# Weight loads from the fourth pair on go to ScalarE's DMA queue, each behind the cast of another pair

## Chip, core and metric

The kernel runs on one core of a Trainium2 chip. The metric is the device time of one execution in microseconds, the median of three runs. All times below are microseconds unless marked otherwise. TensorE is PE in the rows, VectorE DVE, ScalarE ACT, GpSimd POOL and SyncE SP.

## What is computed

A windowed attention, a gated MLP behind an RMS norm, and a second MLP, on 2304 tokens of 512 features (the reference, cut):

```python
scores = (1 / sqrt(D)) * q @ k.T                    # 4 batches, 8 heads, 576 positions, D = 64
scores = where((rel >= 0) & (rel < 64), scores, -1e9)
attn = exp(scores - max); attn = attn / (sum(attn) + 1e-9)
x = (attn @ v) as [2304 tokens, 512]
xn = x / sqrt(mean(x * x) + 1e-6) * rms_g
g = xn @ w_gate; val = xn @ w_val                   # 512 x 1536
x = (g * sigmoid(g) * val) @ w_out                  # 1536 x 512
h = x @ w_in; out = (h * sigmoid(1.702 * h)) @ w_out2   # 512 x 2048, 2048 x 512
```

The weights lie in HBM in 64-bit floats; everything else is 32-bit.

## The kernel before

**Blocks and passes.** The tokens are cut into blocks of 384 columns (three tiles of 128). The first MLP is made in two passes over half of its 1536 hidden features each; a pass goes through the blocks j = 0 to 5. The first pass also makes the attention of block j+1 while TensorE multiplies for block j: scores (`ps_s`, L271), exps (L301), transposes (`ps_t`, L321) that ScalarE copies to `pt` (L233), the product with v (`ps_v`, L336), then the norm (`ps_r`, L367 to L377), and at the end of the block the split of x into a high part `xh` (L385, L387) and a low part `xl` (L389). Each product of the MLPs is made of three passes of high and low parts (L396 for gate `psg`, value `psv` and `psh`; L531 and L622 into `acc`).

**Weights.** A weight chunk of 128 columns is 512 KB in HBM. Two chunks make a pair, and 34 pairs are used in a fixed order (`w_order`): gate and value of one feature chunk, the same of the next, the output rows of both, and so on, then the second MLP. Pairs are numbered from 0 here, so the fourth pair is pair 3. A pair goes through these steps:

- `w_load`: two DMAs of 512 KB into a staging tile `st` (three buffers). L117.
- `w_step`: ScalarE scales the two halves of the words (L144, L145), VectorE joins them into `m` (L146, L147, L150). There is one `m`.
- `w_half`, called at the start of the next step: ScalarE casts `m` to the high part of `w` (L128), VectorE subtracts to get the low part (L129).

In block 0 of the first pass nine pairs are prepared, one behind the other, since every weight is needed for the first time; later blocks and passes prepare the rest beside TensorE's work.

**Who issues loads.** Every DMA of the kernel is issued by SyncE, in one order: loads of q, k and v (L206), weight loads (L117), the store of x (L424), and at the end of a block four stores `o` of the block's result (L607) from two staging tiles `x2s` (ScalarE L606 for columns 0 and 2, VectorE L604 for 1 and 3), so the third `x2s` waits until the first store has landed. The first three pairs are loaded early, from `load_some`. The load of pair i+3 is called in `w_step` behind the join of pair i, and its staging tile is the one that the join of pair i has just read: it waits for that L150. What stands behind it in SyncE's order waits too, and it waits for what stands ahead.

**Order of the work.** A scheduler that knows the tiles, their buffers and the calls of `issue_after` writes out each engine's order when the program is built. Each engine then runs its own order and waits on semaphores.

Of the kernel before, what the change touches and what calls it, by code (L numbers as in the profile page):

```python
# [8 lines left out]
F32 = mybir.dt.float32  # L9
# [13 lines left out]
def window_attention__gated_mlp__mlp_kernel(  # L23
# [13 lines left out]
    nc = tc.nc  # L37
# [61 lines left out]
    w_next = [0, 0]  # L99
# [3 lines left out]
    def w_src(kind, f):  # L103
        c = slice(f * 128, (f + 1) * 128)
        if kind in "gvh":
            w = {"g": w_gate, "v": w_val, "h": w_in2}[kind]
            return w[:, c].bitcast(I32).rearrange("(k p) f -> p k f", p=128)
        return {"o": w_out, "p": w_out2}[kind][c, :].bitcast(I32)

    def w_load(limit):  # L110
        while w_next[0] < min(limit, n_w):
            pair = w_order[w_next[0]]
            w_next[0] += 1
            st = stp.tile([128, 2, 1024], I32, tag="st", name="st")
            for e, (kind, f) in enumerate(pair):
                dst = st[:, e, :].rearrange("p (k f) -> p k f", k=KC) if kind in "gvh" else st[:, e, :]
                nc.sync.dma_start(out=dst, in_=w_src(kind, f))  # L117
            staged.append(st)

    def after(ins):  # L120
        return tc.issue_after(ins) if ins is not None else nullcontext()

    def w_half():
        if not half:
            return
        pair, w24 = half.pop()
        w = wp.tile([128, 2, 1024], F32R, tag="w", name="w")
        nc.scalar.copy(w[:, 0, :], w24.bitcast(F32))  # L128
        nc.vector.tensor_tensor(w[:, 1, :], w24.bitcast(F32), w[:, 0, :].bitcast(F32), ALU.subtract)  # L129
        for e, key in enumerate(pair):  # L130
            weights[key] = w[:, :, e * 512:(e + 1) * 512]

    def w_step(limit):
        w_half()
        if w_next[1] >= min(limit, n_w):
            return
        w_load(w_next[1] + 1)
        pair = w_order[w_next[1]]
        w_next[1] += 1
        st = staged.pop(0).rearrange("p e (f two) -> p (e f) two", two=2)  # L140
        lo, hi = st[:, :, 0], st[:, :, 1]
        m = tmp.tile([128, 1024], I32, tag="tmp", name="m")
        with after(hold[0]):
            nc.scalar.mul(hi.bitcast(F32), hi.bitcast(F32), 2.0 ** -112)  # L144
            nc.scalar.activation(lo, lo.bitcast(U32), AF.Copy, scale=2.0 ** -29)  # L145
        nc.vector.tensor_scalar(m.bitcast(U32), hi.bitcast(U32), 3, None, ALU.logical_shift_left)  # L146
        nc.vector.scalar_tensor_tensor(  # L147
            m.bitcast(U32), hi.bitcast(U32), 0x80000000, m.bitcast(U32), ALU.bitwise_and, ALU.bitwise_or
        )
        nc.vector.tensor_tensor(m, m, lo, ALU.add)  # L150
        half.append((pair, m))
        w_load(w_next[1] + 2)


    NLD = 4
# [24 lines left out]
    def load_some():  # L180
        while ld_next[0] < len(ld_order):
            i = ld_next[0]
            if i >= N_FIRST + NLD and ld_order[i - NLD] not in ld_done:
                return
            kind, m = ld_order[i]
            ld_next[0] += 1
            if N_FIRST <= i <= N_FIRST + 2:
                w_load(i - N_FIRST + 1)
            if i < N_FIRST:
                t = part_tile().rearrange("p (h d) -> p h d", h=H)  # L190
            else:
                t = at.tile([128, H, D], F32, tag="qkv", name="qkv", bufs=NLD)
            ld_tile[kind, m] = t
            if kind == "v":
                if m == 0:
                    nc.vector.memset(t[64:128], 0.0)
                    rr = [(0, 64, 0, 0)]
                elif m % 4 == 0:
                    rr = [(64 * e, 64) + divmod((m - e) * GB, S) for e in range(2)]
                else:  # L200
                    rr = list(runs((m - 1) * GB, 128))
            else:
                rr = list(runs(m * 128, 128))
            src = {"q": q, "k": k, "v": v}[kind]
            for off, n, b, s in rr:
                nc.sync.dma_start(out=t[off:off + n], in_=src[b, :, s:s + n, :].rearrange("h s d -> s h d"))  # L206
# [264 lines left out]
    if True:  # L471
# [30 lines left out]
        for m in range(T0 // 128):  # L502
            att_S(m)
            if m + 1 < T0 // 128:
                att_Tk(m + 1)
                att_Tq(m + 1)
        hold[0] = last_exp[0]
        w_step(1)
        for m in range(T0 // 128):
            att_PT(m)  # L510
# [10 lines left out]
        for ps_i in range(2):  # L521
            f_lo, f_hi = ps_i * FH, (ps_i + 1) * FH
            for j in range(NB):
# [15 lines left out]
                def extras(f, i):  # L539
                    s = 3 * (f - f_lo) + i  # L540
                    if ps_i == 0:
                        for fn in slots.pop(j * NS + s, ()):
                            fn()
                        if j == 0:
                            if s % 2 == 0:
                                w_step(n_wh)
                        elif s % 9 == 8:
                            w_step(n_w1)
                    elif not end:
                        if s % 9 == 2:  # L550
                            w_step(n_w)
                    else:
                        w_step(n_w)
# [141 lines left out]
```

## Time and profile before

| | |
|---|---|
| time, median of 3 runs | 1029.68 (1028.36 to 1031.18) |
| time of the profiled execution | 1027.21 |
| its span | 1025.4 |
| mean granted clock of TensorE | 0.979 |
| TensorE busy | 987.4 (96%) |
| VectorE busy | 517.4 (50%) |
| ScalarE busy | 408.7 (40%) |
| moved by the one DMA queue of the kernel | 87.44 MB |

The span is the time from the first to the last instruction of the profiled execution; its time is 1.8 longer for what lies around it. Busy shares are means over stages that differ: block 0 of the first pass ends at about 125, the first pass with attention runs to about 350, and the rest is matmuls with little beside them.

### The profile page before, as it was taken

To read this page: it belongs to the slowest core of one execution; us is meant where nothing else is said; L and a number is where in the kernel's file an instruction comes from. 1 tells how busy PE (TensorE), PEld (TensorE's weight loads), DVE (VectorE), ACT (ScalarE), POOL (GpSimd) and SP (SyncE) were. 2 spreads that over 40 slices of the span, in tenths; PEclk is the share of its full clock that TensorE was granted. 3 is DMA by queue.
4 is the path that set the end of the run, shared out by engine and by line. 5 is a ranking of instruction groups with operands and counts; after the bars stand their busy time and mean duration, and the time that the engine had idled before them with its cause. 6 is when DMAs were issued, how large, how long until landed. Compare 5 with 4: busy or idle time off the path is not lost.

```text
span 1025.4 us, 15454 instructions
## 1 busy us (share of the span) xinstructions
PE 987.4 (96%) x6158; PEld 917.1 (89%) x6158; DVE 517.4 (50%) x1132; ACT 408.7 (40%) x884; POOL 12.2 (1%) x39
## 2 busy tenths in 40 slices
PE   7888999999989999999999999999999999999997
PEld 5877798988989899999999998998989989999996
DVE  5597756655575655656543688332232322322222
ACT  7586654654554333333332365222222222322222
POOL 2000000000000000000000000000000000000000
PEclk9698999999999999999999999999999999999999
DMA  9648644444361512423411352010010000000000
GB/s 233 184 124 212 181 102 133 101 86 135 83 186 42 196 66 87 165 72 122 157 72 63 113 171 77 1 62 1 1 62 1 32 31 1 31 1 1 32 1 31
DMA packets 113320, 88.43 MB, mean 86 GB/s; under 512 B 77664, under 2 KB 104288, under 8 KB 113248
## 3 DMA queue, kind: packets, MB, share of 16 engines
q1 hardware_dynamic: 113248, 87.44, 29.4%
q8 instruction: 48, 0.79, 0.3%
q14 instruction: 24, 0.20, 0.1%
HBM read 68.55 MB, written 18.87 MB: 85 GB/s over the span
## 4 chain that ended last, share of the span: by engine, by line
PE 83%; DVE 6%; ACT 5%; DMA 4%; issue 1%; SPq 0%; POOL 0%; DVEq 0%; ACTq 0%
PE acc L622 20%; PE psh L396 19%; PE acc L531 13%; PE psg L396 12%; PE psv L396 12%; PE ps_s L271 2%; PE ps_v L336 2%; ACT p L301 1%; PE ps_t L321 1%; DMA st<-in_moe_w_in_dram 1%; DMA st<-in_moe_w_val_dram 1%; DVE xraw L377 1%; ACT st L145 1%; DMA o<-x2s 1%; PE ps_r L367 1%
## 5 line engine op out<-in xcount | busy, mean ns | idle before, releaser
L638 DVE TENSOR_TENSOR a<-a,psh 128x384 f32<-128x384 f32 x96 | 53.0, 553 | 201.9 <-ACT a L637 201.9
L396 PE MATMUL psh<-x2h,w 128*128 128x384 f32 x768 | 153.3, 339 | 0.9 <-DVE a L638 0.6
L622 PE MATMUL acc<-w,gh 128*128 128x512 f32 x576 | 152.9, 397 | 0.0
L396 PEld LDWEIGHTS psh<-x2h,w 128*128 128x128 f32 x768 | 137.2, 188 | 4.3 <-DVE a L638 0.9
L637 ACT ACTIVATE a<-psh 128x384 f32<-128x384 f32 x96 | 47.0, 491 | 220.4 <-PE psh L396 217.2
L622 PEld LDWEIGHTS acc<-w,gh 128*128 128x128 f32 x576 | 107.1, 188 | 18.5
L531 PE MATMUL acc<-ah,w 128*128 128x384 f32 x576 | 117.6, 344 | 3.6 <-ACT w L128 3.3
L531 PEld LDWEIGHTS acc<-ah,w 128*128 128x128 f32 x576 | 103.5, 190 | 4.9 <-ACT w L128 3.7
L565 DVE SCALAR_TENSOR_TENSOR a<-a,psg 128x384 f32<-128x384 f32 x72 | 39.7, 552 | 115.5 <-ACT a L562 115.3
L396 PE MATMUL psh<-x2l,w 128*128 128x384 f32 x384 | 86.2, 338 | 0.0
L622 PE MATMUL acc<-w,gl 128*128 128x512 f32 x288 | 85.1, 396 | 0.0
L642 DVE TENSOR_TENSOR gl<-a,gh 128x384 fp32r<-128x384 f32 x96 | 53.4, 557 | 50.5 <-ACT gh L641 42.7
L562 ACT ACTIVATE a<-psg 128x384 f32<-128x384 f32 x72 | 35.1, 487 | 107.7 <-PE psg L396 107.7
L396 PEld LDWEIGHTS psh<-x2l,w 128*128 128x128 f32 x384 | 69.9, 188 | 5.9
L641 ACT CAST gh<-a 128x384 fp32r<-128x384 f32 x96 | 49.3, 513 | 62.5 <-DVE a L638 49.7
L396 PE MATMUL psg<-xh,w 128*128 128x384 f32 x288 | 65.3, 357 | 6.4 <-DVE a L565 2.6
L622 PEld LDWEIGHTS acc<-w,gl 128*128 128x128 f32 x288 | 54.2, 189 | 12.5
L531 PE MATMUL acc<-al,w 128*128 128x384 f32 x288 | 64.8, 343 | 0.0
L572 ACT CAST ah<-a 128x384 fp32r<-128x384 f32 x72 | 36.8, 511 | 70.1 <-DVE a L569 69.9
L396 PE MATMUL psv<-xh,w 128*128 128x384 f32 x288 | 62.9, 346 | 0.0
L396 PEld LDWEIGHTS psg<-xh,w 128*128 128x128 f32 x288 | 51.3, 193 | 11.4 <-DVE a L565 3.6
L301 ACT ACTIVATE p<-p,sm 128x128 f32<-128x128 f32 x128 | 49.6, 391 | 23.6 <-DVE sm L289 23.6
(104 smaller groups left out, 1433.6 us busy)
## 6 DMA issues: line engine op xcount, KB each, us to landing
st<-in_moe_w_out_dram SPq DMA_DIRECT2D x28, 512.0 KB, 4.3
o<-x2s SPq DMA_DIRECT2D x48, 192.0 KB, 3.4
st<-in_moe_w_in_dram SPq DMA_DIRECT2D x16, 512.0 KB, 5.0
st<-in_moe_w_gate_dram SPq DMA_DIRECT2D x12, 512.0 KB, 4.9
st<-in_moe_w_val_dram SPq DMA_DIRECT2D x12, 512.0 KB, 5.6
qkv<-in_v_dram SPq DMA_DIRECT2D x20, 256.0 KB, 4.2
x<-xraw SPq DMA_DIRECT2D x6, 768.0 KB, 4.7
xr<-x SPq DMA_DIRECT2D x6, 768.0 KB, 4.4
```

Source lines behind the costliest of these rows:

```text
L271: prev = nc.tensor.matmul(banks[e][64 * g:64 * g + 64, hp * 128:(hp + 1) * 128], QT[64 * e:64 * e + 64, hp, 64 * g:64 * g + 64], KT[64 * e ...
L301: last_exp[0] = nc.scalar.activation(p[e][:, hp, :], p[e][:, hp, :], AF.Exp, bias=sm[:, 0, i:i + 1], scale=-1.0, accum_out=sm[:, 1, i:i + ...
L396: nc.tensor.matmul(ps[:, :T], w[:, wi, c * 128:(c + 1) * 128], xx[:, c, :T], start=(i == 0), stop=(i == 3 * KC - 1),)
L531: nc.tensor.matmul(acc[c][:, :T], w[:, wi, c * 128:(c + 1) * 128], aa, start=(f == f_lo and pi == 0), stop=(f == f_hi - 1 and pi == 2),)
L562: tanh = nc.scalar.activation(a, psg[:, :T], AF.Tanh, scale=0.5).ins
L565: nc.vector.scalar_tensor_tensor(a, a, 1.0, psg[:, :T], ALU.add, ALU.mult)
L572: nc.scalar.copy(ah, a)
L622: nc.tensor.matmul(acc[c], (gh, gh, gl)[pi][:, c * 128:(c + 1) * 128], w[:, (0, 1, 0)[pi], :], start=(f == 0 and pi == 0), stop=(f == NF2 ...
L637: nc.scalar.activation(a[:, :T], psh[:, :T], AF.Sigmoid, scale=1.702)
L638: nc.vector.tensor_tensor(a[:, :T], a[:, :T], psh[:, :T], ALU.mult)
L641: nc.scalar.copy(gh[:, :T], a[:, :T])
L642: nc.vector.tensor_tensor(gl[:, :T], a[:, :T], gh[:, :T].bitcast(F32), ALU.subtract)
```

## The change

`w_load` takes a queue. Inside `w_half`, the load of the next pair is called behind the cast (L128), with ScalarE's own queue, and `issue_after(cast)` orders the two DMA instructions behind the cast in ScalarE's order; no semaphore of the cast is waited for. The two calls in `w_step` are gone. The first three pairs are loaded as before, so 31 pairs (62 DMAs) move. The cast of pair i and the new load of pair i+3 both wait for the same L150.

```diff
-    def w_load(limit):
+    def w_load(limit, queue=None):
+        queue = queue or nc.sync
         while w_next[0] < min(limit, n_w):
...
-                nc.sync.dma_start(out=dst, in_=w_src(kind, f))
+                queue.dma_start(out=dst, in_=w_src(kind, f))
             staged.append(st)
...
         w = wp.tile([128, 2, 1024], F32R, tag="w", name="w")
-        nc.scalar.copy(w[:, 0, :], w24.bitcast(F32))
+        cast = nc.scalar.copy(w[:, 0, :], w24.bitcast(F32)).ins
+        with tc.issue_after(cast):
+            w_load(w_next[0] + 1, nc.scalar)
         nc.vector.tensor_tensor(w[:, 1, :], w24.bitcast(F32), w[:, 0, :].bitcast(F32), ALU.subtract)
...
         w_half()
         if w_next[1] >= min(limit, n_w):
             return
-        w_load(w_next[1] + 1)
...
         half.append((pair, m))
-        w_load(w_next[1] + 2)
```

Since the scheduler writes the orders anew, other instructions change places too. ScalarE's order in block 0, from the tanh of feature chunk 2 (`a<-psg`) to that of chunk 3, with the cast of pair 4 and the scaling of pair 6 in it. Before:

```order
L562 ACTIVATE a<-psg 128x384
L344 COPY xraw<-ps_v 128x4x128
L128 CAST w<-m 128x1024
L233 COPY KT<-ps_k 128x4x128
L353 ACTIVATE s_836<-xraw 128x512
L233 COPY QT<-ps_q 128x512
L572 CAST ah<-a 128x384
L233 COPY pt<-ps_t 128x512
L562 ACTIVATE a<-psg 128x384
L144 ACTIVATE st<-st 128x1024
L145 ACTIVATE st<-st 128x1024
L233 COPY pt<-ps_t 128x512
```

The same place in the changed program, whose line numbers are one to two higher there (L129 is the cast, L118 a weight load, L146 and L147 the scaling):

```order
L345 COPY xraw<-ps_v 128x4x128
L129 CAST w<-m 128x1024
L118 DMA st<-in_moe_w_gate_dram 128x4x256
L118 DMA st<-in_moe_w_val_dram 128x4x256
L354 ACTIVATE s_836<-xraw 128x512
L234 COPY KT<-ps_k 128x4x128
L234 COPY QT<-ps_q 128x512
L573 CAST ah<-a 128x384
L234 COPY pt<-ps_t 128x512 x2
L146 ACTIVATE st<-st 128x1024
L147 ACTIVATE st<-st 128x1024
L563 ACTIVATE a<-psg 128x384
```

The load of pair 7 stands behind the cast now, both copies to `pt` stand ahead of the scaling, and the tanh of chunk 3 stands behind it.

ScalarE's order at the end of block 2 of the first pass (the end of block 3 reads alike). Before:

```order
L233 COPY QT<-ps_q 128x512
L606 ACTIVATE x2s<-acc_2026 128x384
L128 CAST w<-m 128x1024
L233 COPY pt<-ps_t 128x512 x2
L387 CAST xh<-xraw 128x384
L606 ACTIVATE x2s<-acc_2028 128x384
L387 CAST xh<-xraw 128x384
```

In the changed program:

```order
L234 COPY QT<-ps_q 128x512
L607 ACTIVATE x2s<-acc_2026 128x384
L129 CAST w<-m 128x1024
L118 DMA st<-in_moe_w_gate_dram 128x4x256
L234 COPY pt<-ps_t 128x512
L118 DMA st<-in_moe_w_val_dram 128x4x256
L234 COPY pt<-ps_t 128x512
L607 ACTIVATE x2s<-acc_2028 128x384
L388 CAST xh<-xraw 128x384 x2
```

The second `x2s` stood between the two casts to `xh` and stands ahead of both now; two DMA instructions stand between the cast and the second copy to `pt`.

## Rows read from the trace of the kernel before

**Rows 1.** Waits of TensorE: waiting tile, releaser, total us, times, longest.

```profile
PE ps_s L271 <- ACT pt L233: 4.3, 1, 4.3
PE ps_t L321 <- ACT pt L233: 3.8, 4, 1.0
PE acc L531 <- ACT w L128: 3.3, 1, 3.3
```

**Rows 2.** Windows: stretch, length, busy of PE, PEld, DVE, ACT, POOL, PEclk, DMA, GB/s.

```profile
82.00:92.00 10.00, 7.95 (x74) 7.37 (x76) 6.72 (x23) 9.12 (x24) 0.00 (x0) 0.66 0.34 115
92.00:106.00 14.00, 13.98 (x119) 12.39 (x114) 13.64 (x17) 7.73 (x13) 0.00 (x0) 1.00 0.99 241
226.00:236.00 10.00, 7.80 (x65) 6.15 (x65) 7.90 (x17) 4.38 (x8) 0.85 (x1) 0.83 0.86 240
380.00:1020.00 640.00, 638.62 (x3331) 597.46 (x3329) 271.36 (x461) 197.44 (x347) 0.00 (x0) 1.00 0.16 55
```

**Rows 3.** Timeline of SP's queue, 25:50: start, duration, operation, tile, count.

```profile
25.95 3.60 SPq L473 DMA_DIRECT2D g_sb<-in_moe_rms_g_dram  x1
...
46.47 0.37 SPq L117 DMA_DIRECT2D st<-in_moe_w_gate_dram  x1
```

**Rows 4.** Timeline of ScalarE, 26:32; in brackets idle time ahead and its releaser.

```profile
28.89 0.58 ACT L233 COPY quad<-ps_t 128x512 f32<-128x512 f32 x1 [0.16 <-PE ps_t L321]
31.15 0.63 ACT L353 ACTIVATE s<-xraw 128x512 f32<-128x512 f32 x1 [1.68 <-PE ps_r L367]
```

**Rows 5.** Timeline of TensorE, 45:60.

```profile
46.48 0.34 PE L396 MATMUL psg<-xl,w 128*128 128x384 f32 x1
```

**Rows 6.** Timeline of ScalarE, 45.5:59.

```profile
48.45 1.05 ACT L128 CAST w<-m 128x1024 fp32r<-128x1024 f32 x1
...
51.63 1.16 ACT L144 ACTIVATE st<-st 128x1024 f32<-128x1024 f32 x1 [1.28 <-DMA st<-in_moe_w_val_dram]
```

**Rows 7.** ScalarE's instructions of line 233 in 50:60, with semaphore events.

```profile
L233 ACTq EVENT_SEMAPHORE  x1: 17/17/17, 56.3 to 56.3; - x1
L233 ACT COPY KT<-ps_k x1: 580/580/580, 58.1 to 58.1; 128x512 f32<-128x512 f32 x1
```

**Rows 8.** Timeline of VectorE, 70:76.

```profile
70.16 1.22 DVE L150 CUSTOM_DVE_ANT_0 m<-st,m 128x2048 uint16<-128x2048 uint16 x1
```

**Rows 9.** Timeline of SP's queue, 71:76.

```profile
72.18 2.65 SPq L206 DMA_DIRECT2D qkv<-in_v_dram  x4
74.94 0.56 SPq L117 DMA_DIRECT2D st<-in_moe_w_gate_dram  x1
```

**Rows 10.** Timeline of ScalarE, 79:90.

```profile
81.44 1.10 ACT L144 ACTIVATE st<-st 128x1024 f32<-128x1024 f32 x1 [3.36 <-DMA st<-in_moe_w_val_dram]
...
83.43 0.57 ACT L233 COPY pt<-ps_t 128x512 f32<-128x512 f32 x1
83.90 1.05 ACT L128 CAST w<-m 128x1024 fp32r<-128x1024 f32 x1
```

**Rows 11.** Timeline of ScalarE, 165:177 (end of block 1).

```profile
169.76 1.05 ACT L128 CAST w<-m 128x1024 fp32r<-128x1024 f32 x1
```

**Rows 12.** Timeline of SP's queue, 226:236 (end of block 2).

```profile
227.30 0.66 SPq L117 DMA_DIRECT2D st<-in_moe_w_gate_dram  x1
228.01 0.97 SPq L607 DMA_DIRECT2D o<-x2s  x2
```

**Rows 13.** Timeline of ScalarE, 226:235.

```profile
233.87 0.49 ACT L606 ACTIVATE x2s<-acc 128x384 f32<-128x384 f32 x1 [2.01 <-DMA o<-x2s]
```

**Rows 14.** Timeline of TensorE, 227:236.

```profile
231.92 0.49 PE L396 MATMUL psg<-xh,w 128*128 128x384 f32 x1 [0.76 <-ACT xh L387]
...
233.04 1.98 PE L271 MATMUL ps_s<-KT,QT 64*64 64x128 f32 x30 [0.32 <-DVE xraw L377]
```

**Rows 15.** The page's part 6, DMA issues: count, KB each, median us to landing.

```profile
o<-x2s SPq DMA_DIRECT2D x48, 192.0 KB, 3.4
```

**Rows 16.** Timeline of ScalarE, 600:626.

```profile
607.44 1.16 ACT L144 ACTIVATE st<-st 128x1024 f32<-128x1024 f32 x1 [3.54 <-DMA st<-in_moe_w_in_dram]
```

## The prediction, made before the change was run

> **What bounds the kernel now.** I read the busy time by windows first. From 380 to 1020 TensorE is busy 638.62 of 640 us [rows 2], so nothing that changes only when a weight arrives can shorten that stretch, as long as the weight still comes in time. What can be won or lost lies ahead of it, and there I read TensorE's waits: the longest single one is 4.3 us of the scores for ScalarE's copy to `pt`, then 3.3 for the cast of a weight, and four waits of about 1 us for `pt`, 3.8 together [rows 1]. For each I went through the timelines of the engine that is waited for and of SyncE's queue, to see which load stands behind it. The columns to watch there are the start and, in brackets, the idle time and what ended it.
>
> **Where SyncE's order costs something.** Pair 4 was joined at 70.16 + 1.22 = 71.38 [rows 8], so the load of pair 7 could have gone then. It went at 74.94, behind four loads of v that SyncE issued from 72.18 for 2.65 us [rows 9]. ScalarE then sat 3.36 us idle for that load until 81.44, scaled for 2.0 us, copied `pt` at 83.43, and only then TensorE could go on [rows 10]: that is the 4.3 us. I found no other load that SyncE held back for more than one issue of another DMA, so this is the one place where another queue wins time by itself.
>
> **When a load goes in the changed kernel.** The load waits for the same join as the cast ahead of it. Does ScalarE's queue issue it when the cast may start, or when the cast has run? The semaphore event of a copy of line 233 stands at 56.3, and the copy itself ran at 58.1, behind the cast of pair 2 in ScalarE's order [rows 7]. So the sequencer runs ahead of its engine, past a cast that has not run; I take it that it issues a DMA there too. Its issue time (0.37 to 0.66 us each, [rows 3, 9, 12]) then lies beside the cast's 1.05 us [rows 6].
>
> **The parts, in order of time.** Plus is slower.
>
> Pair 3. The load would be issued at about 27.3 on ScalarE. SyncE's own issue of `g_sb` takes from 25.95 to 29.55 [rows 3]. No row shows two queues issuing at once. If they don't disturb each other: 0. If the second must wait: the two issues end at 29.55 + 0.37 + 0.56 = 30.5 (lengths from [rows 3, 9]), ScalarE's two copies of 0.58 behind them end at 31.6 and not at 29.47, and 1.68 of these 2.2 us are idle time now [rows 4]: +0.5. I take the middle, **+0.3**.
>
> Pair 4. SyncE issued it at 46.47 [rows 3]. On ScalarE a tanh stands ahead of the cast, and its product ends at 46.48 + 0.34 = 46.82 [rows 5]: the load goes 0.35 later. At the latest it goes when the cast starts, 48.45 [rows 6]: +2.0. ScalarE waited 1.28 us for this load [rows 6], with the exps, the next tanh and the cast behind it for which TensorE waits 3.3 us [rows 1], so a delay is passed on in full. I take the near end, by rows 7: **+0.4**.
>
> Pair 7. The cast of pair 4 stands behind a copy of `ps_v`, for which the loads of v at 72.18 waited too [rows 9]. So ScalarE issues pair 7 from about 72.3 on, up to 2.6 us earlier than 74.94, but beside the four loads of v. I take a landing 2 us earlier, near 79.4. In the changed order both copies to `pt` stand ahead of the scaling, so the scores no longer wait for it. But the tanh of chunk 3 stands behind the scaling now, and the cast of pair 5 behind that: 79.4 + 2.0 + 0.5 + 1.05 = 82.95, where the cast ended at 84.95 [rows 10] (0.5 for the tanh, after the `x2s` copy of as many elements at 0.49 [rows 13]). The output product needs this cast, so TensorE has a smaller wait in place of the large one. How much of it stays? From 92 to 106 VectorE is busy 13.64 of 14 us [rows 2] with the weight chain (three operations a pair and the subtraction) and the masks of the scores. The end of the block is then set by when that chain starts. It starts about 2.0 earlier, less some 0.3 for a subtraction and masks that come ahead of it now: **-1.7**. Bounds: 0 if the load lands no earlier beside the loads of v; -4.3 if the whole wait goes and VectorE keeps up.
>
> End of block 1. The cast at 169.76 stands right ahead of the copy to `pt` [rows 11] that TensorE waits for, one of the four waits of 1.0 [rows 1]. In the changed order this cast and its load stand behind the exps, well ahead. TensorE's next product still needs the norm's chain through GpSimd, so I take half of the wait, **-0.5** (0 to -1.0).
>
> Ends of blocks 2 and 3. Here the third `x2s` stands ahead of both casts to `xh`. It waits until the first store of the block has landed, now at 233.87 [rows 13], while TensorE took the first `xh` at 231.92 [rows 14]. If the store lands as late as now, the cast follows at 234.3 and TensorE at 234.8: 2.9 later, of which the 0.32 that the scores wait anyway [rows 14] are not lost: +2.6. If it lands a median 3.4 us after its issue [rows 15] at about 228.0 [rows 12]: `x2s` at 231.5, `xh` at 231.9, TensorE at 232.4, +0.5, less 0.32: +0.2. Ahead of the store stands half of a weight pair now, issued at 227.30 [rows 12]; this half and the other go to the other queue, but the same memory traffic is there (240 GB/s in the window, [rows 2]). I take a landing half a microsecond above the median case, **+0.8** at each of the two ends, **+1.6**.
>
> The Trainium skill, "DMA: Bandwidth & Descriptors", section "Queues, rings and completion order", has each queue with rings of its own between which a DMA engine takes turns packet by packet. By that the store would no longer stand behind 512 KB but share with them, and the near end would be the better guess: the sum below would be 1.2 lower. No row of this trace shows two queues of the kernel.
>
> The rest. Later pairs are cast and loaded at the same join as now, with TensorE busy 638.62 of 640 us over them [rows 2]. ScalarE waited 3.54 us for one load at 607.44 [rows 16], so there a late issue would cost something; at the same issue I take 0.
>
> **Sum.** 0.3 + 0.4 - 1.7 - 0.5 + 1.6 = +0.1 us against the profiled execution's 1027.21, which is 2.47 below the median of 1029.68. On the median's scale: 1029.8. A run can be told from no change at about 0.3%, 3.1 us.
>
> **Rivals.**
>
> TensorE keeps the whole 4.3 us (faster). For it: the wait is at one place, and TensorE's mean clock in 82 to 92 is 0.66 of full [rows 2], which is 6.8 us at the lower level of 1.2 GHz in place of 2.4, behind the wait; without the wait that may not fall. TensorE is itself busy 13.98 of 14 us from 92 on [rows 2], so earlier work there counts. Against it: VectorE at 13.64 of 14. Time: 2.6 us below the forecast for the wait, and some 1.5 for part of the clock: 1025.7.
>
> The store lands late and holds the casts to `xh` (slower). Place: ends of blocks 2 and 3; price up to +2.6 each in place of +0.8, 3.6 above the forecast: 1033.4. It decides as soon as the first store lands later than about 233.4 at the end of block 2, 5.4 us behind its issue. For it: it lands at 233.8 now. Against: half a pair that stands ahead of it moves away.
>
> The load goes only when the cast has run (slower). Each load is then 1.05 or more later: pair 4 at 49.5, +2.6 beyond the forecast; at 607.44 another 1 to 2 us. Some 4 in all: 1034. Against it: [rows 7].
>
> Nothing but the issuer changes (no change). The Trainium skill, the same page, section "Issuing engines are not separate DMA queues", says that DMAs of different engines run on the same 16 DMA engines and interleave, and that another issuer only saves sequencer time. Rows 9 agree in so far as what pair 7 loses is sequencer time. Here that means that pair 7 lands as late as now, held up by the loads of v beside it, and that the stores land as late as their bytes need: what is lost at 46 and won at 170 cancel, 1029.7.
>
> **Chances.** The forecast 0.35, nothing changes 0.15, the whole wait won 0.27, the late store 0.13, the late issue 0.10. Faster by over 0.3%: 0.27 and 0.03 of the forecast's own spread, 0.30; slower: 0.13 + 0.10 = 0.23; within 0.3%: 0.47. The forecast's own range, from its terms' bounds taken half way, is 1027.5 to 1032.5. The range for 8 in 10 reaches to the first rival with a little beyond it, and to the second: 1025.0 to 1033.5.
>
> **What would show it.** Right: pair 7's DMAs on ScalarE's queue at 72 to 75 and its scaling near 79.4, with no wait of over 2 us for `pt` after it; the load of pair 4 at about 46.9; the first `xh` at the ends of blocks 2 and 3 some 0.8 us later beside the store's landing; from 380 on the same TensorE share. Wrong: a load that starts at its cast's end; ScalarE standing still at 27 to 30.5 and more than 0.5 us lost there; a clock in 82 to 92 at full; a third `x2s` at 233.9 or later, reckoned from the same block's end.

## The result, and the profile after

The changed kernel takes 1039.74 us (median of 4 runs, 1034.93 to 1043.0), the kernel before 1029.02 beside it. The ratio is 1.0101, 95% interval 1.0069 to 1.0134: it is slower by about 1%, and the prediction, 1029.8 with a range to 1033.5, was wrong. The profiled execution took 1040.01, with a span of 1038.2 and a mean clock of 0.973.

The page of the changed kernel, its engines, its DMA queues (packets, MB, share of the engines), and TensorE's longest waits:

```profile
PE 992.3 (96%) x6158; PEld 922.2 (89%) x6158; DVE 517.5 (50%) x1132; ACT 409.2 (39%) x884; POOL 12.2 (1%) x39
...
q1 hardware_dynamic: 90496, 54.93, 19.6%
q10 hardware_dynamic: 22752, 32.51, 10.0%
...
PE psg L397 <- ACT xh L388: 9.9, 4, 4.8
PE acc L532 <- ACT w L129: 6.8, 3, 4.5
```

The wait for `xh` before:

```profile
PE psg L396 <- ACT xh L387: 2.3, 3, 0.8
```

The span grew by 12.8. TensorE is busy 4.9 us longer with the same 6158 matmuls, as its mean clock of 0.973 in place of 0.979 makes them, and idle 7.9 us longer. In [rows 1] the scores waited 4.3 for `pt`; that is gone. In its place the gate product waits 9.9 for `xh` where it waited 2.3, and the output product 6.8 for a cast weight where it waited 3.3. The loads that moved are 32.51 MB on a queue of their own (q10). The medians differ by 10.7, the two profiled executions by 12.8; what follows divides up the 12.8.

Windows of the changed kernel; the first and last stretch are those of [rows 2], the middle one is the end of block 2, which lies some 5 us later here:

```profile
82.00:92.00 10.00, 6.25 (x20) 5.83 (x20) 7.06 (x24) 8.52 (x23) 0.00 (x0) 0.66 0.51 144
238.00:246.00 8.00, 5.32 (x42) 4.56 (x43) 4.47 (x22) 3.33 (x14) 0.00 (x0) 0.57 0.49 187
380.00:1020.00 640.00, 639.58 (x3349) 600.44 (x3348) 272.33 (x463) 197.33 (x347) 0.00 (x0) 1.00 0.16 56
```

Nothing is lost from 380 on. In 238 to 246 the mean clock of 0.57 means 6.9 of 8 us at 1.2 GHz; at the same place before, 0.83 over 10 us means 3.4 [rows 2].

**Where the time went, by place.** I compare the start of TensorE's first gate product of the fourth feature chunk in blocks 1 to 5 of the first pass (before: 140.90, 198.89, 258.09, 315.39, 361.93) with the same start in another profile. The difference steps from column to column by what the block's end in between costs. The last column is the last product of the second MLP. Each row is one execution, which lies up to 3.6 us off its kernel's median (first_block: 1034.13 against 1030.58), and differences of 1 to 2 us also come and go with places where the clock falls. The ratio is therefore what says whether a kernel is slower, and the columns only where this one execution lost its time.

| kernel | ratio (95% interval) | 1 | 2 | 3 | 4 | 5 | last |
|---|---|---|---|---|---|---|---|
| the change | 1.0101 (1.0069, 1.0134) | +4.2 | +4.7 | +7.6 | +11.1 | +13.3 | +12.8 |
| place_only | 0.9998 (0.9982, 1.0013) | -0.7 | -0.9 | -0.1 | +0.8 | +2.4 | +2.3 |
| queue_only | 1.0041 (1.0021, 1.0060) | +1.4 | +2.0 | +3.7 | +5.8 | +5.2 | +3.7 |
| first_block | 1.0032 (1.0015, 1.0048) | +3.8 | +5.3 | +7.5 | +7.4 | +7.2 | +6.9 |
| later_blocks | 1.0074 (1.0046, 1.0102) | -1.4 | +0.9 | +1.0 | +4.1 | +6.3 | +5.6 |
| x2s_behind | 1.0070 (1.0049, 1.0092) | +1.9 | +3.4 | +5.8 | +6.2 | +8.4 | +7.9 |
| order_alone | 1.0041 (1.0028, 1.0055) | +0.2 | +1.4 | +4.2 | +5.7 | +6.0 | +5.1 |
| queue_x2s | 1.0025 (1.0009, 1.0041) | +5.5 | +6.1 | +6.6 | +8.4 | +7.7 | +6.6 |
| before_x2s | 0.9983 (0.9967, 1.0000) | -1.4 | -2.2 | -1.1 | -0.2 | 0.0 | -0.6 |
| pair8_pool | 1.0086 (1.0058, 1.0114) | +1.4 | +2.4 | +3.6 | +7.2 | +9.5 | +9.0 |
| pair8_sync | 1.0096 (1.0071, 1.0120) | +0.4 | +2.9 | +5.8 | +9.7 | +11.9 | +12.2 |
| all_pool | 1.0269 (1.0244, 1.0294) | +11.3 | +14.5 | +17.0 | +19.5 | +26.0 | +29.8 |
| pair7_alone | 1.0008 (0.9997, 1.0020) | +1.2 | +1.7 | +3.5 | +4.7 | +4.8 | +4.9 |
| first_x2s | 1.0036 (1.0022, 1.0050) | +1.3 | +1.9 | +2.2 | +2.7 | +2.8 | +2.6 |
| pair3_alone | 1.0010 (0.9996, 1.0024) | +1.7 | +1.5 | +3.1 | +3.0 | +3.1 | +2.3 |
| pairs_3_6 | 1.0036 (1.0016, 1.0055) | +4.2 | +4.8 | +5.9 | +5.8 | +5.9 | +5.5 |
| pairs_4_6 | 1.0026 (1.0010, 1.0043) | +3.2 | +3.8 | +3.7 | +4.1 | +4.2 | +3.2 |
| pairs_8_11 | 1.0014 (0.9998, 1.0031) | +1.8 | +1.0 | +1.1 | +1.1 | +2.9 | +2.9 |
| early_call | 0.9963 (0.9950, 0.9977) | -1.1 | -0.9 | -0.9 | -0.9 | -0.8 | -1.7 |

In the change, 4.2 come in block 0 and at its end, then 2.9, 3.5 and 2.2 at the ends of blocks 2, 3 and 4.

**The ends of blocks 2 and 4 in the trace.** The end of block 2: SyncE's queue, the stores' landing (line 608, 225 to 245), ScalarE, TensorE:

```profile
232.86 7.71 SPq L608 DMA_DIRECT2D o<-x2s  x3
...
DMA to landing us min/median/max: 2.2/4.7/6.8
...
239.74 0.49 ACT L607 ACTIVATE x2s<-acc 128x384 f32<-128x384 f32 x1 [4.37 <-DMA o<-x2s]
240.12 0.91 ACT L388 CAST xh<-xraw 128x384 fp32r<-128x384 f32 x2
...
240.68 0.69 PE L397 MATMUL psg<-xh,w 128*128 128x384 f32 x1 [4.83 <-ACT xh L388]
```

The first store is issued at 232.86 and the third `x2s` starts at 239.74, 6.9 later; before, it was 5.9 [rows 12, 13]. The load that stood ahead of it has gone to the other queue, and it lands no earlier. Both casts stand behind that `x2s`, and TensorE waits 4.83 where it waited 0.76 [rows 14]. At the end of block 4 the same `x2s` stands ahead of a tanh:

```profile
359.34 0.49 ACT L607 ACTIVATE x2s<-acc 128x384 f32<-128x384 f32 x1 [2.33 <-PE psg L397]
...
359.73 0.48 ACT L563 ACTIVATE a<-psg 128x384 f32<-128x384 f32 x1
...
360.86 2.37 PE L397 MATMUL psg<-xh,w 128*128 128x384 f32 x7 [1.45 <-DVE a L566]
```

The tanh could have run where the `x2s` runs, 0.4 earlier. TensorE waits 1.45 for it, where it waited 1.1 before; and seven of its matmuls then take 2.37 us, where all eight took 1.68 before. TensorE's mean clock is 0.83 from 355 to 365, and it was 1.00 at the same place before (343 to 353).

**Pair 7 in the trace.** SyncE's queue, ScalarE and its queue (ACTq), TensorE:

```profile
72.18 3.02 SPq L207 DMA_DIRECT2D qkv<-in_v_dram  x4
...
75.95 5.69 SPq L207 DMA_DIRECT2D qkv<-in_q_dram  x1
...
72.52 0.39 ACTq L118 DMA_DIRECT2D st<-in_moe_w_gate_dram  x1
72.95 0.66 ACTq L118 DMA_DIRECT2D st<-in_moe_w_val_dram  x1
...
73.80 1.04 ACT L129 CAST w<-m 128x1024 fp32r<-128x1024 f32 x1
...
82.30 1.10 ACT L146 ACTIVATE st<-st 128x1024 f32<-128x1024 f32 x1 [4.18 <-DMA st<-in_moe_w_val_dram]
82.41 0.83 ACTq L118 DMA_DIRECT2D st<-in_moe_w_out_dram  x2
...
85.75 0.69 PE L532 MATMUL acc<-ah,w 128*128 128x384 f32 x1 [4.46 <-ACT w L129]
```

The load is issued before its cast starts (72.52 and 72.95, the cast 73.80), as predicted, and 2.4 us earlier than [rows 9]. ScalarE has it at 82.30, 0.9 later than [rows 10]. Part of that is older: the join of pair 4, here and then in pair8_pool (below), ends at 72.48, 1.1 later than [rows 8]. Counted from that join the scaling starts 9.8 later, and 10.1 before.

```profile
71.25 1.23 DVE L152 CUSTOM_DVE_ANT_0 m<-st,m 128x2048 uint16<-128x2048 uint16 x1
```

```profile
72.13 1.23 DVE L152 CUSTOM_DVE_ANT_0 m<-st,m 128x2048 uint16<-128x2048 uint16 x1
```

The DMA engines from 72 to 86, before and in the change: a larger busy share (0.97 in place of 0.83) and fewer bytes a second (199 GB/s in place of 225).

```profile
72.00:86.00 14.00, 9.18 (x83) 7.82 (x78) 8.92 (x13) 8.86 (x15) 0.00 (x0) 0.86 0.83 225
```

```profile
72.00:86.00 14.00, 8.15 (x83) 7.08 (x78) 9.04 (x15) 9.21 (x15) 0.00 (x0) 0.95 0.97 199
```

### The profile page after: what moved, and what is told of

The parts are those of the page before. It is cut to its first block, busy times and chain, and to the rows that moved or that the text cites. A ratio compares the mean times of both kernels' runs of the same rounds, so it can differ in the third digit from the quotient of the medians.

```text
span 1038.2 us, 15415 instructions
## 1 busy us (share of the span) xinstructions
PE 992.3 (96%) x6158; PEld 922.2 (89%) x6158; DVE 517.5 (50%) x1132; ACT 409.2 (39%) x884; POOL 12.2 (1%) x39
## 3 DMA queue, kind: packets, MB, share of 16 engines
q10 hardware_dynamic: 22752, 32.51, 10.0%
## 4 chain that ended last, share of the span: by engine, by line
PE 81%; DMA 6%; ACT 4%; DVE 4%; SPq 2%; issue 1%; ACTq 0%; POOL 0%; DVEq 0%
PE acc L623 19%; PE psh L397 19%; PE psg L397 13%; PE acc L532 13%; PE psv L397 12%; SPq L207 2%; DMA o<-x2s 1%; PE ps_s L272 1%; DMA st<-in_moe_w_val_dram 1%; PE ps_v L337 1%; ACT p L302 1%; DMA st<-in_moe_w_out_dram 1%; DMA st<-in_moe_w_in_dram 1%; DMA g_sb<-in_moe_rms_g_dram 1%; ACT st L146 1%
## 5 line engine op out<-in xcount | busy, mean ns | idle before, releaser
L397 PE MATMUL psg<-xh,w 128*128 128x384 f32 x288 | 68.5, 372 | 13.6 <-ACT xh L388 9.9
L397 PEld LDWEIGHTS psg<-xh,w 128*128 128x128 f32 x288 | 54.8, 205 | 18.5 <-ACT xh L388 11.1
```

The lines of the kernel that those rows point to most:

```text
L397: nc.tensor.matmul(ps[:, :T], w[:, wi, c * 128:(c + 1) * 128], xx[:, c, :T], start=(i == 0), stop=(i == 3 * KC - 1),)
```

## The experiments

Theory 1 was that the loss comes from ScalarE's one order: the load of pair 8 (82.41 above) stands behind a wait for pair 7, and the third `x2s` stands ahead of casts and tanh. Rival A was that two queues share the engines, rival B that it is the place behind the cast.

**The place or the queue.** Against the change, the call behind the cast on SyncE:

```diff
-            w_load(w_next[0] + 1, nc.scalar)
+            w_load(w_next[0] + 1)
```

> The call sits behind the cast as in the change, but SyncE issues every load. ScalarE's order at the ends of blocks 2 to 4 is that of before. Theory 1 (ScalarE's one order: the load of pair 8 waits behind the scaling of pair 7, and the third x2s waits for a store ahead of the casts and the tanh): no loss, 1029 +- 3. Rival A (two queues share the engines): 1029 too. Rival B (it is the place behind the cast, whoever issues): about 1040.

Against the kernel before, the calls where they were, on ScalarE:

```diff
-                nc.sync.dma_start(out=dst, in_=w_src(kind, f))
+                (nc.sync if w_next[0] <= 3 else nc.scalar).dma_start(out=dst, in_=w_src(kind, f))
```

> The calls stay where they were in the step, but ScalarE's queue issues the loads from the fourth pair on. ScalarE's order at the ends of blocks 2 and 3 becomes that of the change; at the end of block 4 the third x2s stays behind the tanh. Theory 1: the loss of the change less the 2.2 us of the end of block 4, 1037 to 1038. Rival A: 1040, the whole loss. Rival B: 1029.

place_only is the time of before (0.9998): rival B falls. queue_only is slower, 1.0041, but less than expected: its ends of blocks 2 and 3 cost 1.7 and 2.1, and that of block 4, where the tanh stands ahead of the `x2s`, nothing (-0.6).

**First and later blocks.** Against the change:

```diff
-            w_load(w_next[0] + 1, nc.scalar)
+            w_load(w_next[0] + 1, nc.scalar if w_next[0] < 12 else nc.sync)    # first_block
+            w_load(w_next[0] + 1, nc.scalar if w_next[0] >= 12 else nc.sync)   # later_blocks
```

> As the change, but ScalarE's queue issues only pairs 3 to 11, all loaded in block 0; SyncE issues the later ones. At the ends of blocks 2 to 4 ScalarE's order is that of before. Theory 1: only the loss of block 0, about +4.7 less what the end of block 1 gave back, 1032 to 1034. Rival A: a share by bytes, 9 of 31 pairs, +3, 1032. Rival B: 1040.

> The other half: SyncE issues all loads of block 0, ScalarE's queue pairs 12 on. ScalarE's order at the ends of blocks 2, 3 and 4 is that of the change. Theory 1: the loss of the three ends, +8.5, 1037 to 1038, with first-block times as before. Rival A: a share by bytes, +7. Rival B: 1040.

1.0032 and 1.0074: together 1.0106, the 1.0101 of the change. The later loads make some two thirds of the loss, and no weight is late there: it lies at the ends. Rival A, which shared the loss out by bytes (+3 and +7), fits these two times as well as theory 1 does.

**The order at the ends.** Against the change (x2s_behind), queue_only (queue_x2s), first_block (first_x2s) and the kernel before (before_x2s), the same edit:

```diff
-                        split_x(x, nxh, nxl, T)
+                        xcast = split_x(x, nxh, nxl, T)
...
-                        nc.scalar.mul(st, acc[c][:, :T], 0.5)
+                        with after(xcast if c == 2 and not end else None):
+                            nc.scalar.mul(st, acc[c][:, :T], 0.5)
```

> The change, with the third x2s of blocks 0 to 4 ordered behind the last cast to xh on ScalarE; queues and loads as in the change. At the end of block 4 it still stands ahead of the tanh. Theory 1: the ends of blocks 2 and 3 lose their 6.4 us, the rest of the loss stays: 1033 to 1034. Rival A (the stores and loads share the engines, whatever the order): 1040.

> The kernel of queue_only, with the third x2s ordered behind the last cast to xh. Theory 1: the 3.8 us that its profile lost at the ends of blocks 2 and 3 come back, 1028 to 1030. Rival A: no difference to queue_only, 1033.

> The kernel of first_block (ScalarE's queue for pairs 3 to 11 alone) with the third x2s ordered behind the last cast to xh, at the end of block 0 above all, where its profile lost 2.3 us from the start of block 1 to its second chunk. If the order there is the cause: 1028 to 1029, like before. If it is TensorE's clock or the two queues: 1031 to 1033 as first_block.

> The kernel before with the third x2s of blocks 0 to 4 behind the last cast to xh, every load on SyncE. Theory 1: the second cast is not needed before TensorE is done with the scores, so nothing is won: 1028 to 1030.

order_alone goes the other way: the kernel before, all loads on SyncE, with both casts put behind the third `x2s` at the ends of blocks 2 and 3 (VectorE's casts and the store of x move behind it in the program too; SyncE's order there stays that of before):

```diff
-                        split_x(x, nxh, nxl, T)
-                        x_store(j + 1, x)
+                        if j not in (2, 3):
+                            split_x(x, nxh, nxl, T)
+                            x_store(j + 1, x)
...
-                        nc.scalar.mul(st, acc[c][:, :T], 0.5)
+                        third = nc.scalar.mul(st, acc[c][:, :T], 0.5).ins
...
+                    if ps_i == 0 and j in (2, 3) and c == 2:
+                        split_x(x, nxh, nxl, T, third)   # its casts: with after(third)
+                        x_store(j + 1, x)
```

> The kernel before, every load on SyncE, with one thing ordered otherwise: at the ends of blocks 2 and 3 both casts to xh stand behind the third x2s on ScalarE, as in the change. Theory 1 (the order at the ends costs, no second queue needed): 2 to 3 us at each of the two ends, 1033 to 1035. Rival A (two queues): 1029.

order_alone loses 0.41% without a second queue, 2.8 and 1.6 us at the two ends. Its end of block 2, ScalarE and TensorE:

```profile
235.83 0.49 ACT L608 ACTIVATE x2s<-acc 128x384 f32<-128x384 f32 x1 [3.79 <-DMA o<-x2s]
236.21 0.92 ACT L388 CAST xh<-xraw 128x384 fp32r<-128x384 f32 x2
...
236.77 0.69 PE L397 MATMUL psg<-xh,w 128*128 128x384 f32 x1 [4.25 <-ACT xh L388]
```

That is the picture of the change, 4.25 in place of 4.83. The reverse edit gave less. x2s_behind is at 1.0070 against the change's 1.0101, half of what was expected, and the two intervals overlap; queue_x2s is at 1.0025 against queue_only's 1.0041, with overlapping intervals too, where all of the 3.8 us were to come back. By place, the end of block 3 in x2s_behind went from 3.5 to 0.4, but that of block 2 only from 2.9 to 2.4. There the late store reaches TensorE by VectorE, whose own `x2s` waits for a store ahead of its cast to `xh`:

```profile
238.61 0.56 DVE L605 TENSOR_SCALAR x2s<-acc 128x384 f32<-128x384 f32 x1 [1.54 <-DMA o<-x2s]
239.08 0.35 DVE L386 CAST xh<-xraw 128x384 fp32r<-128x384 f32 x1
...
239.49 1.15 PE L397 MATMUL psg<-xh,w 128*128 128x384 f32 x5 [1.02 <-DVE xh L386]
```

Over all profiles the end of block 3 separates the orders: with the `x2s` ahead of the casts it costs 1.6 to 3.9 (six kernels), else -0.1 to 1.2, with two exceptions, queue_x2s at 1.7 and all_pool (below) at 2.5. The end of block 4 costs 2.1 to 2.3 in the change and the four kernels of its order there, and -0.6 to 0.2 in the others but three (1.6 in place_only, 1.8 in pairs_8_11, and all_pool). The end of block 2 does not: later_blocks, with the order of the change, lost 0.1 there. In the six kernels with the `x2s` ahead of the casts the loss at the end of block 2 goes with the landing of the block's first store: 4.6, 5.0, 5.1, 6.1, 6.6 and 6.8 us after its issue (later_blocks, pair8_pool, queue_only, order_alone, pair8_sync, the change) for a loss of 0.1, 1.2, 1.7, 2.8, 2.9 and 2.9. That is what a wait for this store would do. So the order at the ends costs time by itself; how much of the change's loss there comes from the second queue (rival A) stays open. first_x2s is no better than first_block, so the order is not what block 0 loses. before_x2s is not clearly different from before.

**Pair 8.** Against the change, one pair on another queue; every other row stands where it stood:

```diff
-            w_load(w_next[0] + 1, nc.scalar)
+            w_load(w_next[0] + 1, nc.gpsimd if w_next[0] == 8 else nc.scalar)   # pair8_pool
+            w_load(w_next[0] + 1, nc.sync if w_next[0] == 8 else nc.scalar)     # pair8_sync
```

> The change, with the two DMAs of pair 8 alone issued by GpSimd's queue, in which nothing waits; all other orders are the same row for row. Theory 1: pair 8 is issued near the end of its join at about 80 in place of 82.4, lands about 2 us earlier, and block 0 ends 2 us earlier: 1037 to 1038, at the start of block 2 the offset is 2 to 3 in place of 4.7. Rival A: pair 8 shares the same engines and lands as late: 1040.

> The same with SyncE issuing pair 8, behind its load of q, whose issue lasted from 75.95 to 81.64 in the change. Theory 1: 81.7 in place of 82.4, so almost nothing is won: 1039 to 1040. If it is won all the same (1037 to 1038), SyncE's long issue came from something that this edit takes away.

The intervals of both hold 1.0101. In pair8_pool GpSimd issues the load at 81.63, 0.8 earlier only. Its scaling, first in pair8_pool and then in the change, stands right behind the exps, with no wait for a load:

```profile
89.20 1.16 ACT L146 ACTIVATE st<-st 128x1024 f32<-128x1024 f32 x1
```

```profile
90.48 1.17 ACT L146 ACTIVATE st<-st 128x1024 f32<-128x1024 f32 x1
```

The half of theory 1 that blamed pair 8's wait falls: what holds the scaling back is its place behind the exps.

**GpSimd's queue for all.** Against the change, `nc.gpsimd` in place of `nc.scalar`:

> The change, with every load from the fourth pair on issued by GpSimd's queue behind the cast's wait, none by ScalarE. The scheduler then puts the third x2s behind both casts at the ends of blocks 0 to 3. Theory 1: neither loss arises, 1026 to 1030. Rival A (two queues that share): 1036 to 1040.

1.0269, the slowest of all. GpSimd's queue at pair 4:

```profile
49.03 0.79 POOL L118 DMA_DIRECT2D st<-in_moe_w_gate_dram  x1 [8.12 <-DVE m L152]
53.49 0.76 POOL L118 DMA_DIRECT2D st<-in_moe_w_val_dram  x1 [3.68 <-issue]
```

The second half of a gate and value pair goes 4.5 us behind the first, so this run tests neither theory: it measures GpSimd's issue.

**Which loads of block 0.** Against place_only, ScalarE's queue for pair 7, 3 to 6, 8 to 11, 3, and 4 to 6 alone:

```diff
-            w_load(w_next[0] + 1)
+            w_load(w_next[0] + 1, nc.scalar if w_next[0] == 7 else nc.sync)   # pair7_alone; the others alike
```

> The call behind the cast as in place_only, and ScalarE's queue only for pair 7, the one load that SyncE held back behind loads of v. Theory 1: it lands about as late as before, since it shares the engines with these loads, and the rest stays: 1027 to 1031. If a load that is issued 2 us earlier lands 2 us earlier, as the prediction had it: 1026 to 1027.

> ScalarE's queue for pairs 3 to 6 alone, SyncE for the rest. If the loss of the first block comes from loads that share the engines with q, k and v (pair 7 on): 1028 to 1030, like place_only. If it comes from the first loads (a later start of pair 4 and 0.5 at pair 3): 1031 to 1033.

> ScalarE's queue for pairs 8 to 11 alone. If the loads behind pair 7 make the loss at the end of block 0: 1031 to 1033; if not: 1028 to 1030.

> ScalarE's queue for pair 3 alone; apart from its two DMAs every order is that of place_only. If the second queue at the start makes the loss of pairs_3_6 (ScalarE held at 27 to 28.5 beside the issue of g_sb): 1031 to 1033. The prediction priced this at 0 to 0.5 us: 1029 to 1030.

> ScalarE's queue for pairs 4 to 6 alone. ScalarE's order from pair 5 on changes with it: the scaling of pair 8 moves behind the masks and exps, as in pairs_3_6. If pair 4's later issue and that order make the loss: 1031 to 1033. If pair 3 makes it: 1029.

pair7_alone against place_only tests the step on which the predicted gain rested. By time nothing is won: 1.0008 and 0.9998. place_only, SyncE's queue and ScalarE:

```profile
73.91 0.56 SPq L118 DMA_DIRECT2D st<-in_moe_w_gate_dram  x1
74.53 0.50 SPq L118 DMA_DIRECT2D st<-in_moe_w_val_dram  x1
...
75.67 2.11 SPq L207 DMA_DIRECT2D qkv<-in_q_dram  x1
...
80.80 1.10 ACT L146 ACTIVATE st<-st 128x1024 f32<-128x1024 f32 x1 [3.82 <-DMA st<-in_moe_w_val_dram]
```

pair7_alone, ScalarE's queue, SyncE's queue and ScalarE:

```profile
71.16 0.48 ACTq L118 DMA_DIRECT2D st<-in_moe_w_gate_dram  x1
...
71.67 0.78 ACTq L118 DMA_DIRECT2D st<-in_moe_w_val_dram  x1
...
74.88 5.74 SPq L207 DMA_DIRECT2D qkv<-in_q_dram  x1
...
81.22 1.14 ACT L146 ACTIVATE st<-st 128x1024 f32<-128x1024 f32 x1 [5.69 <-DMA st<-in_moe_w_val_dram]
```

Issued 2.9 us earlier, pair 7 is there 0.4 later. But this is one execution, the slowest of its kernel's ten, and the other profiles do not all agree. ScalarE's queue has pair 7 in nine of them, and its second half lands 9.3 to 9.5 us after its issue in three (the change, queue_x2s, pair7_alone) and 6.3 to 7.4 in six (queue_only, first_block, x2s_behind, pair8_pool, pair8_sync, first_x2s). pair8_pool has the change's program up to there; its ScalarE queue and ScalarE:

```profile
74.01 0.52 ACTq L118 DMA_DIRECT2D st<-in_moe_w_val_dram  x1
...
80.95 1.16 ACT L146 ACTIVATE st<-st 128x1024 f32<-128x1024 f32 x1 [1.93 <-DMA st<-in_moe_w_val_dram]
```

In the six the scaling starts 7.0 to 8.1 after the join of pair 4, against 10.1 before, and block 1's first gate product 43.0 to 45.1 after it, against 45.5. In the three it is 9.8 to 11.1, and 46.6 to 46.9. What decides between the two is open. Of the others, pair 3 alone (two DMAs are its whole difference to place_only) gives 1.0010 and is not told from no change; pairs 4 to 6 give 1.0026, and 3 to 6 give 1.0036, all that first_block loses.

The loss begins ahead of pair 7. From the end of the join of pair 3 to that of pair 4 it is 7.2 us in all nine profiles in which SyncE issues pairs 4 to 6, and 7.9 to 9.1 in the ten in which ScalarE does. VectorE's order differs there: in none of the nine, and in all of the ten, a mask of the scores, which waits for TensorE, stands ahead of the subtraction of pair 3. place_only, then pairs_4_6, up to the join of pair 4:

```profile
64.23 1.23 DVE L132 TENSOR_TENSOR w<-m,w 128x1024 fp32r<-128x1024 f32 x1 [1.11 <-ACT w L129]
65.38 0.28 DVE L290 CUSTOM_DVE_ANT_0 p<-ps_s,masks 128x128 f32<-128x128 f32 x1
...
69.08 1.22 DVE L152 CUSTOM_DVE_ANT_0 m<-st,m 128x2048 uint16<-128x2048 uint16 x1
```

```profile
66.06 0.29 DVE L290 CUSTOM_DVE_ANT_0 p<-ps_s,masks 128x128 f32<-128x128 f32 x1 [2.86 <-PE ps_s L272]
66.27 1.22 DVE L132 TENSOR_TENSOR w<-m,w 128x1024 fp32r<-128x1024 f32 x1
...
70.87 1.23 DVE L152 CUSTOM_DVE_ANT_0 m<-st,m 128x2048 uint16<-128x2048 uint16 x1
```

No run has this order without the queue, so it is read from the trace and not tested.

**One queue, called earlier.** In the kernel before, the load of pair i+3 is called behind the join of pair i+1, not of pair i as said above; it waits for the tile of pair i all the same. Against before_x2s, one step earlier:

```diff
-        w_load(w_next[1] + 2)
+        w_load(w_next[1] + 3)
```

> All loads on SyncE, and the load of a pair called one step earlier in the program, so that pair 7 stands ahead of three of the four loads of v in SyncE's order; the third x2s stands behind the casts to xh as in before_x2s. It should land 2 to 3 us earlier, as the prediction wanted of the second queue, since nothing shares the engines with it, and the wait of 4.3 us for the copy to pt should shrink. Theory 1: 1024 to 1027, faster than both kernels. If the wait only moves to the next load: 1027 to 1029.

0.9963 (0.9950 to 0.9977), faster than both kernels. Not by much at pair 7, however. Its SyncE queue, ScalarE, and TensorE's longest wait:

```profile
73.64 0.50 SPq L117 DMA_DIRECT2D st<-in_moe_w_val_dram  x1
...
80.56 1.14 ACT L144 ACTIVATE st<-st 128x1024 f32<-128x1024 f32 x1 [3.75 <-DMA st<-in_moe_w_val_dram]
...
PE ps_s L271 <- ACT pt L233: 4.4, 2, 3.8
```

Issued 1.9 earlier than before, the load is there 0.9 earlier, and the wait of 4.3 becomes 3.8. The rest of its gain is not told apart from that of before_x2s, with whose interval its own overlaps.

## Why the prediction was wrong

**The sum.** Predicted were -1.0 for block 0 (0.3 + 0.4 - 1.7), -0.5 for the end of block 1, +1.6 for those of blocks 2 and 3, and 0 for the rest. The profile shows +4.2, +0.6, +6.4, and for the rest +2.2 at the end of block 4 and -0.5 behind it.

**When a load is issued: right.** Pair 4 goes at 46.98 (about 46.9 predicted), pair 7 at 72.5, both ahead of their casts' start. The rival in which a load waits for its cast falls.

**Pair 7, -1.7: wrong in this execution.** The step that failed is "I take a landing 2 us earlier, near 79.4". The scaling started at 82.30, and from the join of pair 4 to the first gate product of block 1 the change took 46.6 in place of 45.5: +1.1. The loads of v ran beside it on the same engines: the four landed 4.2 to 9.6 us after their issue, and 2.8 to 4.3 before. pair7_alone shows the same with nothing else changed. In six of the nine profiles, however, the landing came as I took it (8.0 after the join of pair 4, measured 7.0 to 8.1), and that stretch was 0.4 to 2.5 shorter than before: the term is a gain that an execution may or may not have. My worst bound, 0, left the second case out. The rival "nothing but the issuer changes", given 0.15, rested on the Trainium skill, "DMA: Bandwidth & Descriptors", section "Issuing engines are not separate DMA queues", by which DMAs of all issuers interleave on the same 16 engines. The change's trace agrees for pair 7: the loads of v and of the weights both took longer from issue to landing (pair 7's second half 9.3 in place of 5.8), and 2.4 us of issue time saved brought no earlier landing. The rival's time, 1029.7, did not come out. The copies to `pt` did move ahead, so the wait went from the scores to the output product, 4.46 in place of 4.3.

**Ends of blocks 2 and 3, +0.8 each: the mechanism was right, the size was not.** They cost 2.9 and 3.5 in the profile. The step that failed is the landing: I took half a microsecond above the median of all stores, 3.4 [rows 15]; the first store at the end of block 2 took 5.8 before and 6.8 in the change. That is the rival of the late store, which I priced at 2.6 each and gave 0.13. The clock adds to it: TensorE's idle stretch of 4.83 is followed by 6.9 us at 1.2 GHz. The Trainium skill, "DMA: Bandwidth & Descriptors", section "Queues, rings and completion order", has engines take turns between the rings of different queues, and by that I called the near end the better guess. The runs do not show such a gain: the first store at the end of block 2 took 4.6 to 6.8 in the seven profiles with these weights on ScalarE's queue and 4.7 to 6.1 in the twelve with them on SyncE's. Nor do they show that it lands later by the second queue. order_alone shows that the order by itself makes such a loss; in x2s_behind's profile it goes at the end of block 3 when the order is undone, and hardly at that of block 2, where VectorE waits for the store.

**"The rest ... I take 0": wrong at the end of block 4.** There the `x2s` got ahead of a tanh: 0.4 us of idle time and a fall of the clock behind it, 2.2 together. I had compared the orders at two ends and not at the third. No run changes this order alone, and in place_only and pairs_8_11 the clock fell there without it, so that the order brings the fall about is not shown.

**Block 0 and its end.** The terms for pairs 3 and 4 were +0.7; the join of pair 4 ends 1.1 later in the change. I had looked at ScalarE's order there and not at VectorE's; in the change's profile the subtraction of pair 3 waits besides for its cast, which stands behind a scaling that waited 2.13 for pair 5. With the 1.1 of pair 7 that makes some 2.2 of the 4.2. The other 1.9 come between the first and the fourth gate product of block 1, for which I had no term: it is 0.9 to 3.1 in all twelve kernels in which ScalarE's queue has any of the pairs 4 to 11, and -0.1 to 0.3 in the seven others (all_pool aside). By which step is open. In the change the third `x2s` stands ahead of both casts to `xh` here too, and TensorE waits 1.0 for them. The clock falls there in ten of the twelve and in none of the seven (in the change its mean is 0.57 from 118 to 126, which is 6.9 of 8 us at 1.2 GHz), but first_x2s loses 1.4 there at full clock and with the `x2s` behind the casts. Nor is it pair 8's place behind the exps alone: early_call has that too and loses nothing up to there (-1.1). The expected -0.5 at the end of block 1 was +0.6.

## What to carry to other kernels

An earlier issue is not an earlier landing: with loads of v beside it, pair 7 landed 9.3 us after its issue in one execution and 6.9 in another with the same program up to there. Look at what moves in the window, and take more than one profile before a term rests on a landing. Where a scheduler writes the orders anew, compare the orders of every engine that feeds TensorE, at every place where an instruction that waits for a DMA or another engine stands in them, and price that wait from the same instruction's own row, not from a median over all of its kind. An edit that only reorders (order_alone) tells in one run whether an order by itself makes such a loss; whether it is all of the loss takes the reverse edit too, which here gave back half of what was expected.

## What the hardware showed that I had not expected

SyncE's issue of the q load behind four loads of v takes 3.06 to 5.74 us in the nine profiles in which ScalarE's queue has pair 7 (5.69 in the change, 5.74 in pair7_alone), and 1.25 to 2.39 in the ten in which SyncE has it (2.11 in place_only): a second queue made the first one's issue slower. And in all_pool GpSimd needs 4.5 us between the two DMAs of this gate and value pair, though each is listed with 0.8; over the run it is 4.3 to 7.1 for such pairs, and 0.5 to 0.6 for the two DMAs of output rows.
